# SyncE's transfers wait for the landing of earlier ones: an attention and maxout kernel on one core

## The chip, the core and the metric

The kernel runs on 1 core of one Trainium2 chip. Its time is in device microseconds; the median of 3 runs of the kernel before is 358.42 us (358.3 to 359.15). Five engines work side by side: TensorE (PE, with its weight loads as PEld), VectorE (DVE), ScalarE (ACT), GpSimd (POOL) and SyncE (SP), which here only issues transfers (DMAs).

## The reference

```python
def _attn_ref(q, k, v):                      # 8 batches, 8 heads, 1152 places, 64 wide
    q_pool = q.reshape(B, H, S // 2, 2, D).mean(axis=3)
    scores = scale * np.matmul(q_pool, k.transpose(0, 1, 3, 2))
    scores = scores - np.max(scores, axis=-1, keepdims=True)
    attn = np.exp(scores)
    attn = attn / (np.sum(attn, axis=-1, keepdims=True) + 1e-09)
    return np.matmul(attn, v)

def _moe_ref(x, w1, w2, w_out):              # x: 4608 tokens x 512, d_ff 1024
    return np.maximum(x @ w1, x @ w2) @ w_out
```

The attention's heads are put side by side as x, and the second function's result, 4608 x 512 in float32, is the output.

## The kernel before

The 64 heads are worked in 32 pairs. For each pair three loads of 576 KB come from HBM: q, k and v, each into one of three buffers (`qraw`, `kraw`, `vraw`). GpSimd casts them to bf16 (`cast_k`, `cast_q` with the pooling's addition, `cast_v`). K is turned by TensorE for the first five pairs (`ktrans_pe`) and by a transposing DMA after that (`ktrans`, line 475); the pooled q is turned by TensorE for the first five pairs and by eight VectorE transposes after that (`qtrans_dve`, line 485). TensorE makes the scores (line 302), ScalarE the exponentials (line 317), TensorE the product with V (line 621). The normalized result is turned into `xT`, for most pairs by a transposing DMA (`xtrans`, lines 703 and 712).

The second part works on `xT` while the attention of later pairs goes on. max(a, b) is computed as b + max(a - b, 0): the weights' difference `wd` is made once, the relu of x @ wd comes out of lines 760 and 771, and x @ (w2 w_out) and the relu's product with w_out are added in one accumulation (line 803). The output tiles are stored by `store_p` (lines 829 and 835), the last ones by `store_z` (line 866). The twelve weight blocks of 512 KB are loaded in the opening (`w_load`, line 379), between the loads of the first pairs.

The order of all work is written out by hand in a long string. Each letter is one step: "S" a group of scores, "E" an exponential, "l" the next load of the list `LOADS`, "t" a `ktrans`, "x" an `xtrans`, "o" a store, and so on. `Plan` records the steps with what they read and write, works out which semaphores each has to wait for (`solve`), and emits each engine's instructions in that order. SyncE, too, works in order: an issue that waits holds up everything behind it. `solve` drops a wait for something of which the engine has already been told by an earlier wait.

What an issue on SyncE waits for today: its buffer being free, its data being there (transposes and stores), and, for loads once the exponential steps are past group 42, an exponential two groups back (`pace`). The function `behind` could make a load wait for an earlier load, but its table is empty:

```python
BEHIND = ()
back = [d for at, d in BEHIND if at <= n]
return [f"ld{n - back[-1]}"] if back else [], [f"ld{n}"]
```

So `behind` only gives the load a name, and nobody waits for that name. Two of the pieces in which k of pair 0 is loaded are issued by ScalarE; all other transfers but some of the last stores are SyncE's.

Of the kernel before, what the change touches and what calls it, by code (L numbers as in the profile page):

```python
# [7 lines left out]
P = 128  # L8
# [8 lines left out]
class Plan:  # L17
# [10 lines left out]
    def op(self, eng, fn, r=(), w=(), after=(), dma=None, fence=False, **_):  # L28
        n = len(self.ops)
        for k in r:  # L30
            assert k in self.writer, k
        raw = {self.writer[k] for k in r}
        deps = set(raw)
        for k in tuple(w) + tuple(after):
            if k in self.writer:
                deps.add(self.writer[k])
            deps.update(self.readers.get(k, ()))
        self.ops.append(dict(eng=eng, fn=fn, deps=deps, raw=raw, dma=dma, fence=fence))
        for k in r:
            self.readers.setdefault(k, set()).add(n)  # L40
        for k in w:
            self.writer[k] = n
            self.readers[k] = set()
        return n
# [72 lines left out]
def bass_funnel_attn__then__act_maxout2_kernel(  # L117
# [13 lines left out]
    NT = S // P  # L131
    HP = P // 2
    QU = SQ // HP
    NCH = SQ // P
    NB = SQ - NCH * P
# [22 lines left out]
    W_DIFFS_DVE = ()  # L158
    W_CASTS_POOL = ()
    W_PAIRS = (0, 2)  # L160
    BEHIND = ()
    FILL = 28
    FILLS = 16
    PACE = 2
# [31 lines left out]
    with ctx:  # L196
        def sbuf(shape, dt, name):
            return ctx.enter_context(nc.sbuf_tensor(name, list(shape), dt))
# [12 lines left out]
        kbf = [sbuf([P, NT, 2, D], BF16, f"kbf{s}") for s in range(2)]  # L211
# [20 lines left out]
        osb2 = stage[:, NC_ * F:NC_ * F + 4 * E].rearrange("p (s e) -> p s e", s=4)  # L232
        osb = [osb2[:, s, :] for s in range(4)]
# [12 lines left out]
        op = plan.op  # L246

        def rows(half):
            return slice(half * HP, half * HP + HP)
# [35 lines left out]
        def kkeys(i, lo=0, hi=NT):  # L285
            return [f"kT{i % 3}.{t}" for t in range(lo, hi)]
# [44 lines left out]
            return [f"E{g}"] if PACE and g >= PACE_FROM else []  # L331

        done = [0]
        issued = [0]

        def behind():

            n = issued[0]
            issued[0] += 1
            back = [d for at, d in BEHIND if at <= n]  # L340
            return [f"ld{n - back[-1]}"] if back else [], [f"ld{n}"]

        def load_k(i, lo=0, hi=NT, eng="SP"):
            b, h0, s = i // NHP, 2 * (i % NHP), i % 3
            old, name = behind() if eng == "SP" else ([], [])
            op(eng, lambda e: e.dma_start(  # L346
                kraw[s][:, :, lo:hi, :].rearrange("p h t d -> p h (t d)"),
                k[b, h0:h0 + 2, :, :].rearrange("h (p t) d -> p h (t d)", t=NT)[
                    :, :, lo * D:hi * D]),
                after=([f"kraw0.{c}" for c in K0] if s == 0 and hi - lo == NT else []) + pace() + old,  # L350
                w=([f"kraw0.{lo}"] if hi - lo < NT else [f"kraw{s}"]) + name,
                dma=f"d_kp{lo}" if hi - lo < NT else f"d_k{s}",
                cost=0.2 * (hi - lo) + 0.03 if hi - lo < NT else 1.45 + 0.6 * (i == 1), tag=("L", "k", i))

        def load_q(i, lo=0, hi=QU, eng="SP"):
            b, h0, s = i // NHP, 2 * (i % NHP), i % 3
            old, name = behind() if eng == "SP" else ([], [])
            op(eng, lambda e: e.dma_start(  # L358
                qraw[s][:, lo:hi, :, :].rearrange("p u r d -> p (u r d)"),
                q[b, h0:h0 + 2, :, :].rearrange("h (p r) d -> (h p) (r d)", p=HP)[  # L360
                    :, lo * 2 * D:hi * 2 * D]),
                w=([f"qraw0.{lo}"] if hi - lo < QU else [f"qraw{s}"]) + name,
                after=(["qraw0.0", "qraw0.4"] if s == 0 and hi - lo == QU else []) + pace() + old,
                dma=f"d_qp{lo}" if hi - lo < QU else f"d_q{s}",
                cost=1.45 * (hi - lo) / QU + (0.7 if lo else 0.0), tag=("L", "q", i))

        def load_v(i):
            b, h0, s = i // NHP, 2 * (i % NHP), i % 3
            old, name = behind()
            op("SP", lambda e: e.dma_start(  # L370
                vraw[s][:, :, :, :].rearrange("p h t d -> p h (t d)"),
                v[b, h0:h0 + 2, :, :].rearrange("h (p t) d -> p h (t d)", t=NT)),
                w=[f"vraw{s}"] + name, after=pace() + old, dma=f"d_v{s}", cost=1.48, tag=("L", "v", i))

        def w_load(part, c):
            src, dst, key = ((moe_w2, w2f, "w2f"), (moe_w1, w1f, "w1f"), (moe_w_out, wof, "wof"))[part]
            n = 2 if part == 2 else 1
            old, name = behind()
            op("SP", lambda e: e.dma_start(
                dst[:, c * n:(c + 1) * n, :],  # L380
                src.rearrange("(c p) f -> p c f", p=P)[:, c * n:(c + 1) * n, :]),
                w=[f"{key}{c}"] + name, after=old, dma=f"d_w{part}{c}", cost=1.34, tag=("L", "w", part, c))
# [89 lines left out]

        def ktrans(i):
            s, z = i % 2, i % 3
            op("SP", lambda e: e.dma_start_transpose(
                kT[z][:, :, :], kbf[s][:, :, :, :].rearrange("p t h d -> p (t h d)")),
                r=[f"kbf{s}"], w=kkeys(i), dma=f"d_kT{z}", cost=2.4, mode="t", tag=("kt", i))

        def qtrans_dve(i, n):
            s, z = i % 2, i % 3  # L480
# [202 lines left out]
        def place(b, j):  # L683
            if b % 2 == 0:
                return b * SQ + j * P
            return b * SQ + (NB + j * P if j < NCH else 0)

        def under(cts, n0, n1):
            return [f"{key}{ct}" for ct in cts for key, lo, hi in (
                ("w2b", 512, 1536), ("w2T", 1536, 2560), ("w2f", 2560, NTOK)) if n0 < hi and lo < n1]  # L690

        def xkeys(ct, n0, n1):
            return [f"xT.{ct}.{j}" for j in range(n0 // HP, n1 // HP)]

        def xneed(i, part):
            return [f"{('xn', 'xr')[part]}{i // NHP % 2}.{2 * (i % NHP) + k}" for k in range(2)]

        def xtrans(i, part):

            b, ct = divmod(i, NHP)  # L700
            if part == 0:
                n0 = place(b, 0)
                op("SP", lambda e: e.dma_start_transpose(
                    xT[:, ct, n0:n0 + NCH * P].rearrange("p (j x) -> p j x", x=P),
                    xnat[b % 2][:, ct, :, :].rearrange("p j c -> p (j c)")),
                    r=xneed(i, 0), w=xkeys(ct, n0, n0 + NCH * P), after=under([ct], n0, n0 + NCH * P),
                    dma=f"d_x{ct}{b % 2}", cost=1.2, mode="t", tag=("xt", i, 0))
            else:
                n0 = place(b, NCH)
                cts = [j % NHP for j in rests(i)]  # L710
                c0, c1 = cts[0], cts[-1] + 1
                op("SP", lambda e: e.dma_start_transpose(
                    xT[:, c0:c1, n0:n0 + NB],
                    xend[b % 2][0:NB, c0:c1, :].rearrange("p j c -> p (j c)")),
                    r=sum((xneed(j, 1) for j in rests(i)), []),
                    w=sum((xkeys(c, n0, n0 + NB) for c in cts), []), after=under(cts, n0, n0 + NB),
                    dma=f"d_y{ct}{b % 2}", cost=0.3 * len(cts), mode="t", tag=("xt", i, 1))

        def xtrans_pe(i):
# [102 lines left out]
        def store_p(n):  # L822

            lo, o = n * 2 * P, n % 2 * 2
            todo = []
            for half in range(2):
                (b, u), (b1, u1) = [spot(lo + k * P + half * HP) for k in range(2)]
                if b1 == b and u1 == u + 2:
                    todo.append(lambda b=b, u=u, half=half: op("SP", lambda e: e.dma_start(
                        out[b * SQ:(b + 1) * SQ, :].rearrange("(p u) e -> p u e", u=QU)[:, u:u + 3:2, :],  # L830
                        osb2[rows(half), o:o + 2, :]), r=[f"osb{o}", f"osb{o + 1}"],
                        dma=f"d_o{o}", cost=0.8, tag=("O", n)))
                else:
                    for k, (b, u) in enumerate(((b, u), (b1, u1))):
                        todo.append(lambda b=b, u=u, k=k, half=half: op("SP", lambda e: e.dma_start(
                            out[b * SQ:(b + 1) * SQ, :].rearrange("(p u) e -> u p e", u=QU)[u, :, :],
                            osb[o + k][rows(half), :]), r=[f"osb{o + k}"], dma=f"d_o{o + k}", cost=0.4,
                            tag=("O", n)))
            return todo

        def z_job(lo, c0, c1, o, eng):
# [200 lines left out]
```

## Time and profile before

| | |
|---|---|
| median of 3 runs | 358.42 us (358.3, 358.42, 359.15) |
| span of the profiled execution, first to last instruction | 356.4 us |
| what lies around the span, from the median | 2.0 us |
| busy: PE, ACT, DVE, POOL | 346.0, 313.8, 230.1, 151.4 us |
| TensorE clock granted | 0.999 |
| moved by the DMA engines | 84.55 MB, mean 237 GB/s |
| HBM read and written | 62.91 MB and 9.44 MB |

The profile comes from one execution, and a time of that execution apart from its span is not given; the table sets its span against the median of the runs. In the rows below, "SPq" is SyncE's queue of issues: the second number is how long the issue itself took SyncE, not how long the data took. The time to landing is counted from the start of the issue until all of the data have arrived. "Idle before" an engine's row is put down to what came last.

### The profile page before, as it was taken

Reading aid. Unit: us, or ns where it says so; the run is one execution under the profiler, and the core shown is the slowest. Engines: PE = TensorE matmul, PEld = TensorE weight load, DVE = VectorE, ACT = ScalarE, POOL = GpSimd, SP = SyncE. Lnnn points to the kernel's source line nnn. Section 1 sums busy time; section 2 is a strip of 40 time slices with the busy share of each in tenths; the row PEclk is TensorE's granted clock in tenths of the full one; section 3 lists DMA queues with packets and bytes.
Section 4 is the critical chain, followed back from the end, with each engine's and each line's share of the span. In section 5 each row is a group of like instructions: output and inputs, shape, how many; then the busy total and the mean of one; then the engine's idle time right before and its main releaser. Section 6 shows DMA issues by size and latency. Waiting matters only on the chain.

```text
span 356.4 us, 13757 instructions
## 1 busy us (share of the span) xinstructions
PE 346.0 (97%) x6178; PEld 218.5 (61%) x6178; DVE 230.1 (65%) x472; ACT 313.8 (88%) x354; POOL 151.4 (42%) x136
## 2 busy tenths in 40 slices
PE   7889999999899999999999999999999999999996
PEld 5556665656564675656666576556576757448753
DVE  2587589974966867985887677785586875414001
ACT  5999999999999899999999989989999796992431
POOL 2625997554564264355544455227444621010000
PEclk9999999999999999999999999999999999999999
DMA  8999999999989989998999699998999943012215
GB/s 271 403 397 398 370 255 309 280 289 261 293 252 279 315 196 350 237 301 183 278 320 260 153 230 301 237 314 234 224 299 255 267 68 75 17 32 47 61 31 148
DMA packets 76699, 84.55 MB, mean 237 GB/s; under 512 B 48480, under 2 KB 49760, under 8 KB 76640
## 3 DMA queue, kind: packets, MB, share of 16 engines
q1 hardware_dynamic: 75856, 83.15, 87.5%
q8 instruction: 48, 0.79, 0.9%
q10 hardware_dynamic: 784, 0.52, 0.5%
q14 instruction: 11, 0.09, 0.1%
HBM read 62.91 MB, written 9.44 MB: 203 GB/s over the span
## 4 chain that ended last, share of the span: by engine, by line
PE 87%; ACT 9%; DMA 2%; issue 1%; SPq 0%; DVE 0%
PE ps L803 25%; PE ps L621 20%; PE ps L302 19%; PE ps L760 16%; ACT et L317 9%; PE ps L636 3%; PE ps L593 2%; DMA qraw<-in_q_dram 2%; PE ps L846 1%; PE ps L552 0%; PE ps L533 0%; SPq L346 0%; DVE qp L428 0%; SPq L358 0%; PE ps L730 0%
## 5 line engine op out<-in xcount | busy, mean ns | idle before, releaser
L317 ACT ACTIVATE et<-ps 128x1024 bf16<-128x1024 f32 (+1 forms) x336 | 302.4, 1019 | 14.5 <-PE ps L302 9.7
L302 PE MATMUL ps<-qpT,kT 64*128 64x256 bf16 (+7 forms) x1162 | 117.3, 283 | 2.7 <-issue 1.1
L485 DVE STREAM_TRANSPOSE qpT<-qp 32x288 bf16<-32x288 bf16 x216 | 101.4, 469 | 10.4 <-PE ps L302 6.1
L760 PE MATMUL ps<-xT,wd 64*128 64x512 bf16 (+3 forms) x832 | 81.2, 311 | 0.2
L302 PEld LDWEIGHTS ps<-qpT,kT 64*128 64x128 bf16 x1162 | 48.3, 94 | 49.7 <-ACT et L317 11.3
L803 PE MATMUL ps<-wo,stage 64*128 64x512 bf16 x544 | 76.4, 376 | 0.0
L435 POOL TENSOR_TENSOR qp<-qraw 128x576 bf16<-128x576 f32 x30 | 42.1, 1406 | 61.1 <-DMA qraw<-in_q_dram 57.3
L621 PEld LDWEIGHTS ps<-vE,et 128*128 128x128 bf16 x1728 | 54.9, 97 | 13.9 <-ACT et L317 9.3
L621 PE MATMUL ps<-vE,et 128*128 128x65 bf16 x1728 | 60.7, 193 | 0.7 <-issue 0.3
L771 DVE TENSOR_SCALAR stage<-ps 128x1024 bf16<-128x1024 f32 (+3 forms) x41 | 39.7, 970 | 21.1 <-PE ps L760 20.6
L760 PEld LDWEIGHTS ps<-xT,wd 64*128 64x128 bf16 x832 | 35.6, 94 | 22.2 <-PE ps L760 1.9
L405 POOL TENSOR_SCALAR kbf<-kraw 128x1152 bf16<-128x1152 f32 x31 | 35.7, 1153 | 26.3 <-DMA kraw<-in_k_dram 25.6
L803 PE MATMUL ps<-w,xT 64*128 64x512 bf16 x272 | 40.8, 377 | 0.0
L803 PEld LDWEIGHTS ps<-wo,stage 64*128 64x128 bf16 x544 | 26.4, 94 | 20.5
L445 POOL TENSOR_SCALAR vE<-vraw 128x1152 bf16<-128x1152 f32 x24 | 27.4, 1154 | 19.4 <-PE ps L636 10.8
L809 DVE COPY stage<-ps 128x1024 f32<-128x1024 f32 x14 | 17.1, 1224 | 23.1 <-PE ps L803 23.0
L468 POOL TENSOR_SCALAR stage<-et 128x1152 bf16<-128x1152 bf16 x14 | 16.1, 1152 | 35.5 <-ACT et L317 35.5
L654 DVE TENSOR_TENSOR xnat<-ps,rc 128x256 bf16<-128x256 f32 (+2 forms) x71 | 27.6, 397 | 2.0
L651 DVE RECIPROCAL rc<-ps 128x4 f32<-128x4 f32 (+2 forms) x64 | 11.6, 182 | 25.9 <-PE ps L621 25.5
L621 PEld LDWEIGHTS ps<-stage,et 128*128 128x128 bf16 x576 | 18.1, 97 | 2.7 <-issue 2.6
L621 PE MATMUL ps<-stage,et 128*128 128x65 bf16 x576 | 19.7, 193 | 0.0
L803 PEld LDWEIGHTS ps<-w,xT 64*128 64x128 bf16 x272 | 12.5, 94 | 8.8 <-DVE stage L771 0.2
(55 smaller groups left out, 155.4 us busy)
## 6 DMA issues: line engine op xcount, KB each, us to landing
vraw<-in_v_dram SPq DMA_DIRECT2D x32, 576.0 KB, 6.1
kraw<-in_k_dram SPq DMA_DIRECT2D x31, 576.0 KB, 6.7
qraw<-in_q_dram SPq DMA_DIRECT2D x31, 576.0 KB, 6.3
out_dram<-stage SPq DMA_DIRECT2D x24, 256.0 KB, 4.1
out_dram<-stage SPq DMA_DIRECT2D x21, 128.0 KB, 3.4
xT<-in_moe_w_dram SPq DMA_DIRECT2D x4, 512.0 KB, 12.2
stage<-in_moe_w_out_dram SPq DMA_DIRECT2D x4, 512.0 KB, 14.1
stage<-in_moe_w_dram SPq DMA_DIRECT2D x4, 512.0 KB, 13.2
```

The costliest lines, as they stand in the source:

```text
L302: last = e.matmul(ps[:, h, col:col + hi - lo], kT[i % 3][rows(h), t, :], qpT[i % 3][rows(h), lo:hi], start=True, stop=True)
L317: op("ACT", lambda e: e.activation(et2[:, :, c:c + z - a], ps[:, :, a - g * W:z - g * W], EXP, scale=scale), r=[f"b{m}", f"b{m + 1}"], w=w ...
L405: op("POOL", lambda g: g.tensor_scalar(kbf[s][:, :, :, :].rearrange("p t h d -> p h t d"), kraw[r][:, :, :, :], 1.0, 1.0, ALU.mult, ALU.mu ...
L435: op("POOL", lambda g: g.tensor_tensor(qpf[s][:, :, :], qraw[r][:, :, 0, :], qraw[r][:, :, 1, :], ALU.add), r=[f"qraw{r}"], w=[f"qp{s}.0", ...
L445: return g.tensor_scalar(vE[r][:, :, :, 0:D].rearrange("p t h d -> p h t d"), vraw[s][:, :, :, :], 1.0, 1.0, ALU.mult, ALU.mult)
L485: op("DVE", lambda e: e.transpose(view[dst:dst + 32, :, 32 * pb:32 * pb + 32], qpf[s][src:src + 32, :, 32 * db:32 * db + 32]), r=[f"qp{s}. ...
L621: last = e.matmul(fb[m][:, at * 66:at * 66 + 65], et[:, a:a + P], vE[vs][:, t, half, 0:65], start=(t == 0), stop=(t == NT - 1))
L654: todo.append(evac_op("DVE", lambda e, m, z=z, at=at, num=num, dst=dst: e.tensor_tensor(dst, a(m)[z, at:at + num, 0:D], rc[k][z, at:at + n ...
L760: last = e.matmul(fb[m + k][:, 0:size], wd[z, ct, (f0 + k) * P:(f0 + k + 1) * P], xT[z, ct, n0:n1], start=(turn == 0 and ct == 0), stop=(t ...
L771: return e.tensor_scalar_max(gT[:, f0:f0 + 2, g0:g0 + size], wide[m // 2][:, :, 0:size], 0.0)
L803: last = e.matmul(fb[m + k][:, :], lhs, rhs, start=(turn == 0 and j == 0), stop=(turn == 1 and j == NC_ + NF - 1))
L809: return e.tensor_copy(osb2[:, o:o + 2, :], wide[m // 2][:, :, :])
```

## The change

`behind` gets the cost of the transfer it is asked about, in us (1.45 for a load of q, k or v, 1.29 for a weight block, 1.05 for a transpose of K, 0.5 or 0.25 per block for one of x, 0.67 or 0.36 for a store). It goes back through the line of all earlier transfers of SyncE, adding up costs, its own included. The first one at which the sum passes `LINE` = 5.9 and which is not a store is the one whose landing the new transfer has to wait for. Besides the loads, now the DMA transposes and the stores of `store_p` stand in the line and wait in this way; `store_z` does not. The order of the steps, the buffers and all other work are the same.

```diff
-    BEHIND = ()
+    LINE = 5.9
...
-        issued = [0]
-
-        def behind():
-
-            n = issued[0]
-            issued[0] += 1
-            back = [d for at, d in BEHIND if at <= n]
-            return [f"ld{n - back[-1]}"] if back else [], [f"ld{n}"]
+        line = []
+
+        def behind(cost, store=False):
+
+            name, sent, old = f"dm{len(line)}", cost, []
+            for back, c, stores in reversed(line):
+                sent += c
+                if sent > LINE and not stores:
+                    old = [back]
+                    break
+            line.append((name, cost, store))
+            return old, [name]
...
-            old, name = behind() if eng == "SP" else ([], [])
+            old, name = behind(1.45 * (hi - lo) / NT) if eng == "SP" else ([], [])
...
-            old, name = behind()
+            old, name = behind(1.45)
...
-            old, name = behind()
+            old, name = behind(1.29)
...
         def ktrans(i):
             s, z = i % 2, i % 3
+            old, name = behind(1.05)
             op("SP", lambda e: e.dma_start_transpose(
                 kT[z][:, :, :], kbf[s][:, :, :, :].rearrange("p t h d -> p (t h d)")),
-                r=[f"kbf{s}"], w=kkeys(i), dma=f"d_kT{z}", cost=2.4, mode="t", tag=("kt", i))
+                r=[f"kbf{s}"], w=kkeys(i) + name, after=old, dma=f"d_kT{z}", cost=2.4, mode="t", tag=("kt", i))
...
+                old, name = behind(0.5)
...
+                old, name = behind(0.25 * len(cts))
...
+            def store(dst, src, r, dma, cost):
+                old, name = behind(cost, True)
+                op("SP", lambda e: e.dma_start(dst, src), r=r, w=name, after=old, dma=dma,
+                   cost=cost * 1.2, tag=("O", n))
```

More of the change, by code (lines that the diff above doesn't have):

```diff
@@ L356, in load_q @@
             b, h0, s = i // NHP, 2 * (i % NHP), i % 3
-            old, name = behind() if eng == "SP" else ([], [])
+            old, name = behind(1.45 * (hi - lo) / QU) if eng == "SP" else ([], [])
             op(eng, lambda e: e.dma_start(
@@ L705, in xtrans @@
                     xnat[b % 2][:, ct, :, :].rearrange("p j c -> p (j c)")),
-                    r=xneed(i, 0), w=xkeys(ct, n0, n0 + NCH * P), after=under([ct], n0, n0 + NCH * P),
+                    r=xneed(i, 0), w=xkeys(ct, n0, n0 + NCH * P) + name,
+                    after=under([ct], n0, n0 + NCH * P) + old,
                     dma=f"d_x{ct}{b % 2}", cost=1.2, mode="t", tag=("xt", i, 0))
@@ L715, in xtrans @@
                     r=sum((xneed(j, 1) for j in rests(i)), []),
-                    w=sum((xkeys(c, n0, n0 + NB) for c in cts), []), after=under(cts, n0, n0 + NB),
+                    w=sum((xkeys(c, n0, n0 + NB) for c in cts), name),
+                    after=under(cts, n0, n0 + NB) + old,
                     dma=f"d_y{ct}{b % 2}", cost=0.3 * len(cts), mode="t", tag=("xt", i, 1))
@@ L828, in store_p @@
                 if b1 == b and u1 == u + 2:
-                    todo.append(lambda b=b, u=u, half=half: op("SP", lambda e: e.dma_start(
+                    todo.append(lambda b=b, u=u, half=half: store(
                         out[b * SQ:(b + 1) * SQ, :].rearrange("(p u) e -> p u e", u=QU)[:, u:u + 3:2, :],
-                        osb2[rows(half), o:o + 2, :]), r=[f"osb{o}", f"osb{o + 1}"],
-                        dma=f"d_o{o}", cost=0.8, tag=("O", n)))
+                        osb2[rows(half), o:o + 2, :], [f"osb{o}", f"osb{o + 1}"], f"d_o{o}", 0.67))
                 else:
                     for k, (b, u) in enumerate(((b, u), (b1, u1))):
-                        todo.append(lambda b=b, u=u, k=k, half=half: op("SP", lambda e: e.dma_start(
+                        todo.append(lambda b=b, u=u, k=k, half=half: store(
                             out[b * SQ:(b + 1) * SQ, :].rearrange("(p u) e -> u p e", u=QU)[u, :, :],
-                            osb[o + k][rows(half), :]), r=[f"osb{o + k}"], dma=f"d_o{o + k}", cost=0.4,
-                            tag=("O", n)))
+                            osb[o + k][rows(half), :], [f"osb{o + k}"], f"d_o{o + k}", 0.36))
             return todo
```

## The prediction

> **What bounds the kernel now.** I read the page first (busy shares, slices, chain), then the busy times by stage, then who waited for whom, then SyncE's timeline with the landing of single transfers.
>
> ```profile
> span 356.4 us, 13757 instructions
> PE 346.0 (97%) x6178; PEld 218.5 (61%) x6178; DVE 230.1 (65%) x472; ACT 313.8 (88%) x354; POOL 151.4 (42%) x136
> DMA  8999999999989989998999699998999943012215
> PE 87%; ACT 9%; DMA 2%; issue 1%; SPq 0%; DVE 0%
> vraw<-in_v_dram SPq DMA_DIRECT2D x32, 576.0 KB, 6.1
> kraw<-in_k_dram SPq DMA_DIRECT2D x31, 576.0 KB, 6.7
> qraw<-in_q_dram SPq DMA_DIRECT2D x31, 576.0 KB, 6.3
> xT<-in_moe_w_dram SPq DMA_DIRECT2D x4, 512.0 KB, 12.2
> stage<-in_moe_w_out_dram SPq DMA_DIRECT2D x4, 512.0 KB, 14.1
> stage<-in_moe_w_dram SPq DMA_DIRECT2D x4, 512.0 KB, 13.2
> ```
>
> PE works 346.0 of 356.4 us: it leaves 10.4 us in all that any change to the transfers could win. The DMA engines look full too (nines nearly to slice 32), but the chain that ended last has 2% of DMA against 87% of PE. The last number of each transfer row is the median time from issue to landing, and it holds the fact that this change turns on: the loads of the long middle land some 6 us after their issue, the weights of the opening 12 to 14 us after it. So the line is much deeper in the opening than later. The next view gives PE's idle time by stage (columns: length, PE, PEld, DVE, ACT, POOL, then the clock, DMA share and GB/s).
>
> ```profile
> 0.00:9.00 9.00, 6.53 (x92) 5.16 (x92) 2.47 (x8) 4.97 (x6) 1.82 (x11) 1.00 0.81 272
> 9.00:25.00 16.00, 13.70 (x306) 8.18 (x302) 10.72 (x17) 15.57 (x18) 8.32 (x7) 1.00 1.04 398
> 25.00:45.00 20.00, 19.48 (x392) 12.29 (x394) 13.87 (x24) 19.57 (x24) 14.01 (x13) 1.00 1.00 383
> 45.00:60.00 15.00, 14.59 (x250) 8.08 (x246) 13.08 (x28) 14.99 (x18) 13.72 (x12) 1.00 1.16 283
> 60.00:290.00 230.00, 228.47 (x4150) 145.51 (x4152) 171.15 (x361) 220.94 (x247) 110.10 (x92) 1.00 1.04 260
> 290.00:357.00 67.00, 63.23 (x1002) 39.28 (x994) 18.78 (x37) 37.79 (x47) 3.46 (x3) 0.99 0.25 59
> ```
>
> From 60 to 290 us PE idles 1.5 us in 230. From 9 to 60 us ACT is the fuller engine (idle 0.4, 0.4 and 0.0 us). Before 9 us everything waits for the first loads, and after 290 us there are no loads (59 GB/s). So the loads can decide the time in the opening alone, up to about 46 us, where they run at 383 to 398 GB/s. Who waits for them:
>
> ```profile
> POOL qp L435 <- DMA qraw<-in_q_dram: 57.3, 22, 6.2
> POOL kbf L405 <- DMA kraw<-in_k_dram: 25.6, 15, 3.5
> POOL stage L445 <- DMA vraw<-in_v_dram: 10.2, 6, 4.4
> PEld ps L302 <- ACT et L317: 11.3, 48, 0.5
> DVE qpT L485 <- POOL qp L435: 0.8, 3, 0.3
> DVE xT L498 <- DMA xT<-in_moe_w_dram: 0.7, 2, 0.4
> SPq L475 <- POOL kbf L405: 11.9, 2, 10.7
> ```
>
> GpSimd's casts wait for loads all the time (57.3 + 25.6 + 10.2 us), yet DVE, which takes what they make, waits for them 0.8 us in the whole run, and no row of PE or ACT names kT or xT landing late. A load that lands a little later in the middle costs GpSimd time it has (42% busy). In the opening the cover is thin: DVE's weight casts (L498) start when their load lands.
>
> **Part 1: the waits in the opening.** The rule adds up the costs of the transfers ahead until the sum passes 5.9. With 1.45 for a load and 1.29 for a weight block, four later ones fit (4 x 1.45 = 5.8), so a transfer waits for the landing of the fourth or fifth ahead. SyncE's opening today:
>
> ```profile
> 2.24 0.47 SPq L358 DMA_DIRECT2D qraw<-in_q_dram  x1
> 2.75 0.43 SPq L346 DMA_DIRECT2D kraw<-in_k_dram  x1
> 3.23 0.94 SPq L358 DMA_DIRECT2D qraw<-in_q_dram  x2
> 10.84 5.89 SPq L379 DMA_DIRECT2D stage<-in_moe_w_out_dram  x3
> 23.96 4.05 SPq L358 DMA_DIRECT2D qraw<-in_q_dram  x2
> 31.96 0.71 SPq L346 DMA_DIRECT2D kraw<-in_k_dram  x1
> 43.38 1.50 SPq L475 DMA_TRANSPOSE kT<-kbf  x1
> ```
>
> Issue to landing, one row for each: the q load of 2.24, the q load of 26.8 (the second of the pair at 23.96), the k load of 31.96, and for comparison the v load issued at 243.3, ahead of which in the line was only a transpose issued 4.4 us before it:
>
> ```profile
> DMA to landing us min/median/max: 5.9/5.9/5.9
> DMA to landing us min/median/max: 13.3/13.3/13.3
> DMA to landing us min/median/max: 14.8/14.8/14.8
> DMA to landing us min/median/max: 4.1/4.1/4.1
> ```
>
> The fourth transfer lands at 2.24 + 5.9 = 8.1 us and the 31st at 31.96 + 14.8 = 46.8: 27 transfers in 38.7 us, 1.43 us each. So the k load issued at 31.96 has about 14.8 / 1.43 = 10 transfers in the line. SyncE runs far ahead, until the line itself stops it: three weight issues take 5.89 us of its queue.
>
> After the change the first transfer held is the second q load of the pair at 3.23; from there on all 25 up to 31.96 are, the last ones by some 8 us. For the last k load the fourth ahead is the q load of 26.8, which lands at 26.8 + 13.3 = 40.1: it is issued at 40.1 instead of 31.96. What is queued behind it on SyncE is the transpose at 43.38, and that one waits until then for GpSimd's cast anyway (the 10.7 us in the last row of the waits). So the late issue delays nothing behind it.
>
> What it does to landings: when a transfer is released, the three or four ahead of it still have 4 x 1.43 - 1.43 = 4.3 us or more of the line's work, and an unhindered load needs 4.1 us from issue to landing, 1.4 of them its own data. Its data are wanted by the line after 4.3 us, and it needs 4.1 - 1.4 = 2.7 us to begin: 1.6 us of cover. The line's order is the same and it does not run dry, so landings stay where they are. Cost of this part: 0, hidden by those 1.6 us; without them, see the first rival. A gain is excluded before 9 us, because the loads that the opening waits for (those at 0.8 to 3.23) are issued before any wait.
>
> **Part 2: the middle.** The loads land 6.1 to 6.7 us after issue, 4 to 5 transfers at 1.43: the line already stands at the depth that the rule sets, because buffers and exponentials pace the issues. Stepping through all 208 issues that the diff touches with the landing times of the trace, 11 of the later ones would be held, by 0.1 to 1.1 us. The longest, the v load issued at 134.09, would wait for the v load issued at 128.87; their issues and landings:
>
> ```profile
> 128.87 0.63 SPq L370 DMA_DIRECT2D vraw<-in_v_dram  x1
> DMA to landing us min/median/max: 6.3/6.3/6.3
> 134.09 0.44 SPq L370 DMA_DIRECT2D vraw<-in_v_dram  x1
> DMA to landing us min/median/max: 8.1/8.1/8.1
> ```
>
> It is released at 128.87 + 6.3 = 135.2 and lands, as now, at 134.09 + 8.1 = 142.2, since from 135.2 it needs only 4.1 us (139.3). Behind it on SyncE stand a q load, a k load and the transpose of a K; each is in the same position. If the whole 1.1 us did reach the landing, GpSimd would take it, and DVE's 0.8 us of waiting in the whole run shows how seldom that gets further. Cost: 0; bounds 0 and the two places where issues are held in a row (about 134 and 175 us, 1.1 and 0.8 us), so 1.9 us.
>
> **Part 3: the wait instructions.** Up to some 200 waits are added to SyncE, fewer where the planner already knows a landing. The price of one that is met shows in the gap ahead of an issue:
>
> ```profile
> 5.75 0.94 SPq L379 DMA_DIRECT2D xT<-in_moe_w_dram  x2
> 6.81 0.38 SPq L346 DMA_DIRECT2D kraw<-in_k_dram  x1
> ```
>
> The k load at 6.81 waits for the casts of pair 0, long done then: 6.81 - 5.75 - 0.94 = 0.12 us of gap. The k load at 2.75 above has no wait and a gap of 2.75 - 2.24 - 0.47 = 0.04 us. So a met wait costs at most 0.08 us, for some six issues per pair of heads 0.5 us on a queue that then waits for ACT again. It does not add up from pair to pair. The stores of the end get a wait on transfers landed long ago, under 0.1 us each, and the last stores (L866) are not touched. Cost to the end: 0 to 0.1 us, and I take 0.1.
>
> **The sum.** 0 + 0 + 0.1 us: the span stays at 356.4 to 356.5. The median of the runs shown is 358.42, 2.0 us above the profiled span; with that difference kept, 358.5, and I forecast no change: 358.5 us. About 0.3% (1.1 us) is what a measurement of this kernel can tell from no change.
>
> **Rivals.** *Four are too few (slower).* The place is the opening, the mechanism a round trip longer under load than the 4.1 us of the quiet line; it decides from the point where issue to landing exceeds four times 1.43 = 5.7 us. If it were the 6.3 us that q loads take at the median, each transfer would cost 6.3 / 4 = 1.58 instead of 1.43, 0.15 us more; over the some 16 transfers that land up to 32 us and feed weight casts and the first heads that is 2.3 us. ACT has 0.9 us of idle time from 9 to 45 us, so nearly all of it would reach the end: 358.4 + 2.3 = 360.7. For it: DVE's weight cast waits for its load today. Against it: the 6.3 us contain the time behind other loads, at the very depth in question. The Trainium skill (DMA: Bandwidth & Descriptors, Latency and other measured facts) has the memory's latency at 0.2 us on average and 2 us at high load; an estimate by it adds 1.8 us to the quiet 4.1, 5.9 in all, and would put the line just past the point of this rival. No run here shows that latency by itself. The same page's rule for authors to issue early and wait late also speaks for this rival. I give it 0.15.
>
> *The held issues of the middle come through (slower).* The two rows of held issues pass their 1.9 us to the landing of q, and GpSimd's in-order queue passes them to DVE's transposes and these to PE: 358.4 + 1.9 = 360.3. Against it stand 0.8 us of DVE waits; 0.07.
>
> *A shallow line serves better (faster).* Ten transfers in the line might slow the one at its head, or stop SyncE when something urgent comes. It could win part of the 2.3 us that PE idles from 9 to 25 us, say half: 358.4 - 1.2 = 357.2. For it: the issues of up to 5.89 us. Against it: nothing urgent stands in SyncE's queue before 43.38, the order is the same, and 398 GB/s is the highest rate of any stage; 0.12.
>
> *The change does nothing* because the planner drops the waits: in the opening SyncE has waited for almost nothing, so it cannot; it would give the forecast's time anyway.
>
> **How the numbers follow.** No change has 0.66 and lies within 1.1 us, 357.4 to 359.5 with the spread of the runs. The slower rivals have 0.22, the faster 0.12. The range goes from 357.2, the faster rival's time, to 360.7, the first rival's: it leaves out what lies beyond them, under 0.2.
>
> **What would show it.** Right: the issues from 3.7 to 32 us drawn out to 40 us, the weights landing some 6 us after issue instead of 12 to 14, no issue of 5.89 us any more; the last load of the opening still landing near 46.8 us, 383 to 398 GB/s from 9 to 45 us, PE's idle time by stage as above. Wrong in the first way: fewer GB/s from 9 to 45 us and DVE's and GpSimd's casts waiting longer there. Wrong in the second: more than 0.8 us of DVE waiting for qp, and PE idle after 60 us. Wrong in the third: PE over 13.7 us busy from 9 to 25 us with less filling.

## The result, and the profile after

The changed kernel is slower: 360.82 us at the median (359.82 to 362.68) against 358.90 us for the kernel before in the same measurement (357.99 to 359.21). The ratio is 1.0061 with a 95% interval of [1.0038, 1.0084]: about +2.2 us by the ratio, +1.9 us by the two medians. The ratios here and below leave out executions in the chip's slower state (one of "line74" and one of "middle2"), and so they are not exactly the quotients of the medians. The time is the first rival's (360.7), not the forecast's (358.5). A second measurement of the same changed kernel, "after2" below, gave 1.0035 [1.0005, 1.0065]. The profiled execution took 360.82 us at a span of 358.8; as before, 2.0 us lie around the span.

The page of the kernel after (head, summary of the chain of waits, and issues with their median time to landing):

```profile
span 358.8 us, 13826 instructions
PE 345.7 (96%) x6177; PEld 218.5 (61%) x6178; DVE 229.9 (64%) x472; ACT 313.9 (88%) x354; POOL 151.5 (42%) x136
PE 81%; DMA 11%; ACT 5%; issue 1%; POOL 0%; DVE 0%; SPq 0%
vraw<-in_v_dram SPq DMA_DIRECT2D x32, 576.0 KB, 6.0
kraw<-in_k_dram SPq DMA_DIRECT2D x31, 576.0 KB, 6.3
xT<-in_moe_w_dram SPq DMA_DIRECT2D x4, 512.0 KB, 6.2
stage<-in_moe_w_out_dram SPq DMA_DIRECT2D x4, 512.0 KB, 5.8
stage<-in_moe_w_dram SPq DMA_DIRECT2D x4, 512.0 KB, 6.2
```

The weights land some 6 us after issue instead of 12 to 14, as foreseen. PE's work is the same (345.7 us). What is new is DMA's share of the chain that ended last: 11% instead of 2%. The chain in order of time shows where (start, duration, what; the long pieces up to 60 us):

```profile
1.28 3.50 DMA kraw<-in_k_dram
4.80 7.15 DMA qraw<-in_q_dram
11.96 6.59 DMA xT<-in_moe_w_dram
18.57 5.98 DMA vraw<-in_v_dram
24.56 5.94 DMA qraw<-in_q_dram
30.52 6.19 DMA stage<-in_moe_w_dram
36.73 5.73 DMA qraw<-in_q_dram
42.52 1.41 POOL qp L439
45.91 13.43 ACT et L317 x15
```

This is the change at work. Each load starts where the one before it ends: the landing of one releases the issue of the next. The same view of the kernel before has nothing of the kind there; from 9 us on it runs through the exponentials, with short pieces of TensorE's work between the two long rows:

```profile
2.24 5.91 DMA qraw<-in_q_dram
9.43 15.70 ACT et L317 x17
44.70 13.43 ACT et L317 x15
```

Each link of the new chain moves the line on by four transfers, which SyncE's timeline lets one count (start, duration, and the issues in a row without idle time between):

```profile
18.57 0.38 SPq L374 DMA_DIRECT2D vraw<-in_v_dram  x1
20.01 3.46 SPq L383 DMA_DIRECT2D stage<-in_moe_w_out_dram  x3
24.56 0.34 SPq L362 DMA_DIRECT2D qraw<-in_q_dram  x1
...
42.47 0.37 SPq L350 DMA_DIRECT2D kraw<-in_k_dram  x1
45.20 2.10 SPq L480 DMA_TRANSPOSE kT<-kbf  x1
```

From the v load at 18.57 to the q load at 24.56 there are four issues (the v load and three weight blocks). The five links from 11.96 to 42.46 us are 30.5 us for twenty transfers: 1.53 us each on average, where the kernel before took 1.43. The last load of the opening is issued at 42.47 and lands 7.0 us later:

```profile
DMA to landing us min/median/max: 7.0/7.0/7.0
```

That is 49.4 us instead of 46.8, and the transpose behind it is issued at 45.20 instead of 43.38. By stage (columns as in the prediction):

```profile
9.00:25.00 16.00, 12.70 (x297) 7.89 (x296) 10.13 (x15) 15.56 (x18) 7.50 (x7) 1.00 1.00 361
25.00:45.00 20.00, 18.30 (x368) 11.41 (x368) 12.68 (x23) 18.57 (x21) 13.12 (x11) 1.00 1.01 371
45.00:60.00 15.00, 14.71 (x264) 8.50 (x262) 12.93 (x29) 14.68 (x17) 14.65 (x14) 1.00 1.13 302
60.00:290.00 230.00, 227.42 (x4137) 144.79 (x4134) 171.28 (x360) 220.12 (x246) 109.79 (x92) 1.00 1.04 262
```

The rate falls from 398 and 383 to 361 and 371 GB/s. The DMA share goes from 1.04 and 1.00 to 1.00 and 1.01: it counts the time of packets, not bytes, and says little of the loss. ACT, the fuller engine up to 60 us, is busy 53.97 us by then (5.16 from 0 to 9 us, with 15.56 + 18.57 + 14.68) against 55.10 before (4.97 + 15.57 + 19.57 + 14.99): 1.1 us lost. Most of the rest of the 2.4 us between the two spans is in PE's busy time from 60 to 290 us, 227.42 against 228.47. Who waited for whom:

```profile
DVE qpT L490 <- POOL qp L439: 2.6, 2, 2.0
PE ps L302 <- issue: 2.1, 1, 2.1
DVE wo L503 <- DMA stage<-in_moe_w_out_dram: 0.9, 2, 0.7
```

DVE's longest wait for q (2.0 us) lies in the opening, behind the q load that the chain shows at 36.73. So the sign that the prediction named for its second rival (over 0.8 us of DVE waiting for qp) appears, but from the opening. The wait of PE that ends on nothing shown ("issue") is one of 2.1 us near 93 us; it was 1.1 us before. The experiments come back to it.

### The profile page after: what moved, and what is told of

Read it like the earlier page. It is cut to its first block, busy times and chain, and to the rows that moved or that the text cites. A ratio compares the mean times of both kernels' runs of the same rounds, so it can differ in the third digit from the quotient of the medians.

```text
span 358.8 us, 13826 instructions
## 1 busy us (share of the span) xinstructions
PE 345.7 (96%) x6177; PEld 218.5 (61%) x6178; DVE 229.9 (64%) x472; ACT 313.9 (88%) x354; POOL 151.5 (42%) x136
## 4 chain that ended last, share of the span: by engine, by line
PE 81%; DMA 11%; ACT 5%; issue 1%; POOL 0%; DVE 0%; SPq 0%
PE ps L812 25%; PE ps L626 19%; PE ps L302 18%; PE ps L769 16%; DMA qraw<-in_q_dram 5%; ACT et L317 5%; PE ps L641 3%; DMA xT<-in_moe_w_dram 2%; DMA stage<-in_moe_w_dram 2%; DMA vraw<-in_v_dram 2%; PE ps L859 1%; DMA kraw<-in_k_dram 1%; POOL qp L439 0%; PE ps L557 0%; DVE qpT L490 0%
## 5 line engine op out<-in xcount | busy, mean ns | idle before, releaser
L626 PEld LDWEIGHTS ps<-vE,et 128*128 128x128 bf16 x1728 | 54.8, 97 | 13.4 <-ACT et L317 9.0
L449 POOL TENSOR_SCALAR vE<-vraw 128x1152 bf16<-128x1152 f32 x24 | 27.3, 1153 | 20.3 <-DMA vraw<-in_v_dram 11.0
```

Of the source, the lines that this page charges most:

```text
L449: return g.tensor_scalar(vE[r][:, :, :, 0:D].rearrange("p t h d -> p h t d"), vraw[s][:, :, :, :], 1.0, 1.0, ALU.mult, ALU.mult)
L626: last = e.matmul(fb[m][:, at * 66:at * 66 + 65], et[:, a:a + P], vE[vs][:, t, half, 0:65], start=(t == 0), stop=(t == NT - 1))
```

## The experiments

Theory A, after the result: a transfer is released only when its last piece has landed, under load that takes over four times 1.43 us, and so four outstanding transfers starve the line in the opening. The rivals: the loss comes from the middle, from the waiting instructions themselves, or from the wait of PE near 93 us.

**One part alone.** "opening" holds only the first 31 transfers, "middle" only the later ones; "middle2" is the same kernel as "middle", measured anew. The edit of "opening" is shown; in "middle" the condition is `31 <= len(line) < 1000000`.

```diff
-                if sent > LINE and not stores:
+                if sent > LINE and not stores and 0 <= len(line) < 31:
```

> The waits of the change hold only the first 31 transfers of SyncE (up to the last load of the opening); later ones have none. Theory A (the loss is made in the opening: a transfer is released by the last of its sixteen DMA engines, the engines that are 2 us ahead of it run dry, and the stalls that the deep line hid reach the landings): the last load of the opening lands 2 to 3 us later than its 46.7 us, 9 to 45 us run at 360 to 375 GB/s, and the kernel is slower by 1.2 to 2.0 us, nearly all of what the whole change cost. Rival B (the held issues of the middle, or SyncE's time for the waits): landings of the opening late but absorbed, the kernel slower by 0.3 us at most.

> The waits of the change hold only transfers after the first 31; the opening is issued as before. Theory A: opening as before (last load at 46.7 us, 383 to 398 GB/s), the kernel within 0.3 us of before. Rival B: slower by 1.5 to 2 us, PE idle after 60 us.

> The middle alone at 5.9 again, with more runs, since 0.5 us with an interval from 0 to 1.1 us did not settle it. Theory A: 0 to 0.4 us. Rival B: 0.5 to 1.0 us, clear of nothing.

Measured: opening 1.0022 [1.0001, 1.0042] (359.37 us against 358.55); middle 1.0015 [0.9997, 1.0032] (359.27 against 358.55), and anew 0.9999 [0.9970, 1.0028] (359.17 against 358.52). The stages of the kernel "opening":

```profile
9.00:25.00 16.00, 14.72 (x294) 8.76 (x293) 10.09 (x15) 15.00 (x17) 7.08 (x7) 1.00 0.98 356
25.00:45.00 20.00, 19.48 (x406) 12.15 (x401) 13.69 (x26) 19.94 (x24) 12.85 (x11) 1.00 1.02 382
```

and its chain of waits from 9 us on, which is the same ladder of landings:

```profile
12.72 6.88 DMA kraw<-in_k_dram
19.62 6.12 DMA stage<-in_moe_w_out_dram
25.76 5.53 DMA stage<-in_moe_w_out_dram
31.30 6.69 DMA kraw<-in_k_dram
38.02 6.11 DMA kraw<-in_k_dram
```

The kernel "middle" has the opening of before, on its first stage:

```profile
9.00:25.00 16.00, 14.30 (x298) 8.36 (x298) 10.58 (x17) 15.28 (x18) 8.30 (x7) 1.00 1.04 400
```

So the slow line comes with the hold in the opening and with nothing else. The last load of "opening" lands at 49.4 us, 2.6 us late, as expected; its rates (356 and 382 GB/s) lie just outside the expected 360 to 375. In time, the opening alone costs some 0.8 us (the interval goes from near 0 to 1.5), less than the 1.2 to 2.0 expected; the middle costs at most 0.3%, and both of its intervals include no change.

**The waiting instructions without the hold.** LINE = 20 keeps the machinery and lets some fourteen transfers be outstanding.

```diff
-    LINE = 5.9
+    LINE = 20.0
```

> The change with 20 in place of 5.9: the same names, and waits for a transfer some fourteen ahead, which has landed long before except for a moment in the opening, so that nearly nothing is held. Theory A: within 0.3 us of before. Rival C (not the depth costs, but the wait instructions and what the planner makes of them): slower by 1 to 2 us, as the whole change is.

> 20 in place of 5.9 again, the only variant whose median (357.96 us) was under that of the kernel before (358.55 us), with an interval on both sides of no change. If waits that hold almost nothing change nothing: within 0.3 us of before, and its opening as deep as before (weights landing 12 to 15 us after issue). If a bounded but deep line is truly better: faster by 0.5 us or more, clear of nothing.

Measured: 0.9989 [0.9963, 1.0015] and, for the same kernel anew, 1.0020 [0.9998, 1.0041]. The first looked a little faster, the second a little slower; both include no change, and the weights of the opening land 12 to 15 us after issue as before. The waits cost nothing that shows.

**One more outstanding.** LINE = 7.4 adds one load to the line.

> The change with 7.4 in place of 5.9: five transfers outstanding instead of four, one more at 1.43 us. Theory A: an unhindered round trip of 4.1 us and the 2.1 us by which the last engine lands after the first are 6.2 us, less than five times 1.43 = 7.15, so most of the loss is gone: at most 0.5 us slower than before, last load of the opening under 1 us late. Rival D (any limit on the depth costs about the same, since the line served ten deep is served faster): slower by 1.5 us or more, 9 to 45 us still under 375 GB/s.

Measured: 1.0003 [0.9986, 1.0021]. Its first two stages, its weights, and the issue and landing of the last load of the opening:

```profile
9.00:25.00 16.00, 14.10 (x307) 8.40 (x307) 10.85 (x17) 15.63 (x18) 8.02 (x7) 1.00 1.04 399
25.00:45.00 20.00, 19.58 (x408) 12.46 (x407) 13.86 (x24) 19.84 (x24) 13.89 (x13) 1.00 1.00 382
```

```profile
stage<-in_moe_w_out_dram SPq DMA_DIRECT2D x4, 512.0 KB, 7.0
```

```profile
38.61 0.37 SPq L350 DMA_DIRECT2D kraw<-in_k_dram  x1
```

```profile
DMA to landing us min/median/max: 8.1/8.1/8.1
```

The hold is plain to see (weights 7.0 us after issue; last load issued at 38.61 instead of 31.96), yet the rate is that of before and the load lands at 46.7, as before. Five outstanding transfers do what the prediction said that four would do.

**The changed kernel again, and fewer outstanding.** "after2" is the changed kernel. "open44" (LINE = 4.45, the first 31 transfers) leaves three outstanding in the opening, "mid44" (LINE = 4.45, the later ones) three in the middle.

> The changed kernel again, unaltered, with more runs, so that it stands on the same chip as its parts. Holding the opening alone cost 0.8 us and holding the middle alone 0.5 us (that one not clear of nothing). If the two add up and nothing else is in it: slower by 1.0 to 1.6 us, 0.3 to 0.45%. If the parts feed each other (a late opening leaves the middle less slack): 2 us or more.

> 4.45 in place of 5.9, so three outstanding, and only for the first 31 transfers. Theory A (a round trip holds the unhindered 4.1 us and the spread of the engines, some 2 us): a transfer of the opening takes up to 6.1 / 3 = 2.0 us instead of 1.43, and no less than 1.7 if the spread shrinks to 1 us; the last load of the opening lands 6 to 14 us late, the kernel is slower by 4 to 12 us. Rival Q (the spread plays no part, only the unhindered 4.1 us): 4.1 / 3 = 1.37 is under 1.43, so three are about as good as four: last load at most 3 us late, slower by at most 1 us.

> 4.45 in place of 5.9, three outstanding, only for transfers after the first 31. Theory A with the middle's cover as the prediction had it (nothing that PE needs is late by less than some us): within 0.5 us of before, although far more issues are held. Rival B (what is held in the middle comes through): clearly more than the 0.5 us that holding at 5.9 showed, 1.5 us or more, with PE idle between 60 and 290 us and DVE waiting for qp for over 3 us.

Measured: after2 1.0035 [1.0005, 1.0065], open44 1.0203 [1.0151, 1.0255], mid44 1.0123 [1.0086, 1.0159]. after2 is about 1.25 us slower, which fits parts that add up; the first measurement (+2.2 us) fits parts that feed each other. The runs do not decide between the two. The first stage of open44, and issue and landing of its last load of the opening:

```profile
9.00:25.00 16.00, 12.73 (x261) 7.63 (x260) 8.54 (x13) 14.41 (x16) 6.83 (x6) 0.97 0.88 297
```

```profile
49.12 0.37 SPq L350 DMA_DIRECT2D kraw<-in_k_dram  x1
```

```profile
DMA to landing us min/median/max: 5.7/5.7/5.7
```

297 GB/s, and the last load lands at 54.8 us, 8.1 us late: fewer outstanding, slower line, as theory A has it, and rival Q (at most 3 us late) is out. Not all of the time need be the loads': TensorE's granted clock is 0.97 in this stage, and in two of the four runs it is 0.986 over the whole; the one run at 1.00 took 364.82 us, 6.3 us more than the median of before. With mid44 the theory missed: it expected 0.5 us at most and the middle lost 4.4 us, with DVE waiting 3.8 us for qp, as rival B has it. The middle has cover for four outstanding transfers, not for three.

**What a transfer takes from issue to release.** The trace records the completion of each transfer sixteen times, once for each DMA engine, and its waiting instruction needs all sixteen. Worked out from these records for the 25 transfers of the opening from the seventh on (medians in us; "us per transfer" is the mean from the seventh landing to the 31st; a step is the time from one landing to the next, counted up to the 31st landing from the fifth on):

```
kernel (outstanding)   issue to first   issue to last   first to last   us per     steps of        last load
                       engine           engine          engine          transfer   1.9 or more     lands at
before (about ten)     10.96            13.12           2.13            1.43       1               46.7
line74 (five)           4.98             7.05           2.05            1.47       2               46.7
after  (four)           3.94             5.98           2.08            1.56       5               49.4
after2 (four)           4.15             6.25           2.13            1.60       7               50.3
opening (four)          4.17             6.20           2.15            1.59       5               49.4
open44 (three)          3.57             5.21           1.62            1.78       9               54.8
```

The quiet v load of 243.3 had its first engine done 3.27 us after issue and its last 4.09 us after, 0.8 us apart. With four outstanding the first engine is done after 3.9 to 4.2 us, so 0.7 to 0.9 us later than in the quiet line, and the last one some 2.1 us behind it. 6.0 to 6.25 us for four is 1.50 to 1.56 each, more than the 1.43 that the line can do; five fit (7.05 / 5 = 1.41), three are far off (5.21 / 3 = 1.74). In the deep line the engines are as far apart (2.13 us), but nobody waits for that. The loss is not spread evenly: the median step is 1.43 us before and 1.44 and 1.45 us in the two profiles of the changed kernel, and what it loses lies in the few long steps, of up to 2.7 us.

**A stall of one engine.** To see whether delays of single engines add up in a line that waits for the slowest, a transfer of 17 rows (34 KB) that runs on one engine (it leaves two completions in the trace, the others sixteen) was put behind the 13th transfer, in the kernel before ("one_before") and in the changed one ("one_after", "one_after2"). Its data are not used.

```diff
+        def one_engine():
+            op("SP", lambda e: e.dma_start(
+                xnat[1][0:17, 0:2, :, :].rearrange("p a b c -> p (a b c)").bitcast(FP32), moe_w_out[0:17, :]),
+                w=[f"xn1.{h}" for h in range(8)], dma="d_one", cost=0.1)
...
+                if c == "l" and len(sp_line["l"]) == LEFT:
+                    simple["s"].pop(0)()
```

> The kernel before, with one more transfer put into SyncE's line behind the 13th: 34 KB in 17 rows, which go over a single DMA engine and keep it busy some 1.4 us longer than the other fifteen (the data are not used). Theory A (the deep line hides a stall of one engine, since the others do not wait for it and another engine is last anyway): the first engine of each transfer lands as before, the last load of the opening lands within 0.3 us of the 45.9 to 47.2 us seen in the four profiles with a deep opening. Rival E (a stall of one engine delays the landings whatever the depth): all landings from there on 1.0 to 1.4 us later, the load of weights ahead of the last load at 45.3 to 45.7 instead of 44.1 to 44.4 us.

> The changed kernel with the same extra transfer behind the 13th. Theory A (four outstanding: the late engine holds the release of the transfer four behind, and all sixteen engines with it): first and last engine of the transfers from the 18th on land 0.7 to 1.4 us later than in the two profiles of the changed kernel (there the 18th, a weight block, lands at 28.5 and 28.8 us, the last load at 49.4 and 50.3 us). Rival E: the same shift in both kernels. Rival F (a stall of one engine plays no part in either): no shift over 0.5 us.

> The same kernel once more for a second profile, since the landings of the opening differ by up to 0.9 us between the two profiles of the changed kernel. Theory A as before: the mean of the two 0.7 to 1.4 us later than the mean of the two without the extra transfer.

Measured: 0.9997 [0.9936, 1.0058], 1.0047 [0.9983, 1.0111] and 1.0026 [0.9958, 1.0093]; the landings say more. In the kernel before, the last load landed at 46.58, as expected of a stall that is hidden, and as it would without one. In the changed kernel nothing was added either: the 18th transfer landed at 28.1 us in both against 28.5 and 28.8 without, the last load at 48.9 and 48.2 against 49.4 and 50.3. The expectation failed. In "one_after" the small transfer was done at 20.59, between the first engine (18.73) and the last (20.66) of its neighbour: it seems to have taken an engine that had time. So this experiment doesn't show single stalls adding up; what stands is the spread of about 2.1 us itself.

The traces hold candidates of their own, though. The instruction queue (`q8 instruction` on the page) moves 16 KB in a single packet of 1.0 to 1.4 us every 4 to 9 us of the opening. In the kernel before, by the second landing after each of its packets at 12.4, 20.3, 26.5, 32.8 and 40.1 us one more engine is over 1.3 us behind the first (from one engine to six), and the landing itself does not move; only the packet at 44.2 is followed by a long step (2.4 us). In the changed kernel the packets at 10.9, 25.2, 32.0 and 46.0 us are followed within three landings by four of the five long steps (2.7, 2.0, 2.3 and 2.7 us), those at 20.0 and 36.6 us by none. This is read from the times alone; no run tested it.

**The wait of PE near 93 us.** It measured 1.1 us before and 2.1 after, but also 1.1 in opening, line74 and open44, 1.2 in mid44, 1.4 and 1.5 in middle and middle2, 0.9 in line20, and 1.1 and 1.3 in the changed kernel with the extra transfer. The changed kernel's second profile has no such wait of PE on that line; its PE is busy 229.21 us from 60 to 290. So the 1 us that this wait added in the first profile isn't tied to the change. The intervals of the two measurements (+0.6% and +0.35%) overlap; whether this wait has a part in the difference was not shown.

## Why the prediction was wrong

**Part 1, the opening, is the step that failed.** It was costed at 0, under "1.6 us of cover": when a transfer is released the line has 4.3 us of work left, and a load "needs 4.1 - 1.4 = 2.7 us to begin". The 4.1 us came from a load that had the line almost to itself, and the line was treated as one pipe. Held at four, a load took 6.0 to 6.25 us from issue to its last engine (medians), so 4.5 to 4.8 us "to begin" where the prediction had 2.7, and the line had 4.3 us of work: not 1.6 us of cover but 0.3 to 0.5 us short in every four, on average. About 0.8 us of the difference is in the first engine and 1.3 us in the spread between the engines, of which the last one releases the next issue. This sum is the rate told in another way; that the limit is the cause is shown by the runs, with the loss gone at five outstanding and at twenty in LINE, and larger at three. (By the rule it is always the fourth transfer ahead that is waited for, not the fourth or fifth, since a transfer's own cost counts in the sum.) From it follow the other misses of this part: the last load was to be issued at 40.1 and went at 42.5; it was to land near 46.8 and landed at 49.4 and 50.3; 383 to 398 GB/s became 361 and 371. "The late issue delays nothing behind it" fell with it: the transpose went from 43.38 to 45.20.

**How much reaches the end.** The last load of the opening lands 2.7 and 3.6 us late in the two profiles of the changed kernel, and the time grew by 2.2 and 1.3 us. ACT's busy time in the first 60 us is 53.3 to 54.7 us in the five profiles with four outstanding in the opening (53.97, 53.32, 53.61, 53.33, 54.72; mean 53.8) and 54.4 to 55.4 in the eight with five or more (mean 54.9): about 1.1 us, which agrees with the 0.8 us that holding the opening alone cost.

**Part 2, the middle**, was costed at 0 with a bound of 1.9 us, and at four outstanding the runs agree as far as they can tell (1.0015 and 0.9999, at most 0.3%). mid44 shows the edge one step further on, at three.

**Part 3, the waits,** held: line20 stays within no change.

**The gain before 9 us** was excluded, and none came from the change: the loads up to 3.23 us go out as before. PE is busy 7.32 us up to 9 us where the profile of before has 6.53, but 7.49 and 7.20 in middle and middle2, whose opening is not held.

**The first rival** had the place, the condition (a round trip over 5.7 us) and the size per transfer: 6.3 / 4 = 1.58 us against 1.53 to 1.60 measured. That its time, 360.7 us, lies so near 360.8 and 360.3 is in part luck: it let nearly all of its 2.3 us reach the end, and of the 2.6 us by which "opening" lands late about 0.8 us did. It got 0.15 because of the argument that "the 6.3 us contain the time behind other loads, at the very depth in question". That was the wrong way round: at a limit of four, time behind three other loads is part of the round trip. The median of the middle, where four to five were outstanding already, was the nearest row for a line held at four, and the 4.1 us of a quiet line the farthest. The trace of before also held the second half: in its deep line first and last engine were 2.13 us apart.

**The estimate from the Trainium skill** (DMA: Bandwidth & Descriptors, Latency and other measured facts), 5.9 us, came close in sum to the 6.0 to 6.25 measured. The records can't tell whether the memory's latency is in it. Against the quiet load the first engine is 0.7 to 0.9 us later and the last 1.9 to 2.2, so more than half of the difference is spread between the engines. That fits another section of the same page of the Trainium skill (Why a DMA increments its semaphore by 16 and not by 1), by which the engines of one transfer finish independently and only the full count says that all is there.

**Open:** whether the packets of the instruction queue are what sets the engines apart and makes the long steps, why the spread is some 2.1 us with four outstanding as with ten (and 1.6 with three), and the size of the one wait near 93 us. A release by the first engine was not tried, since its data need not all be there.

## What to carry to other kernels

To bound the outstanding transfers, divide the time from issue to the landing of the last engine, measured under load at about that depth, by the time per transfer of the full line, and round up: here 6.2 / 1.43 gives five, and four cost 0.3 to 0.6%. The quiet transfer's time is too short a measure, and the quotient holds only for the depth at which it was taken: with three outstanding it gives four (5.2 / 1.43 = 3.6), which was too few, and in the deep line ten (13.1 / 1.43 = 9.2), which is more than needed. So measure once more at the limit that it gives. Where loads are the pace, as in this opening, read GB/s and the chain in order of time: a ladder of loads, each starting where another ends, is a line that waits for itself.

## What was not expected of the hardware

The sixteen engines of one transfer finish some 2.1 us apart under load, with ten outstanding as with four, and 0.8 us apart in the quiet load. A line of three, four, five and about ten transfers of 512 to 576 KB moved 297, 361, 399 and 398 GB/s in the same stretch, while the DMA share read 0.88, 1.00, 1.04 and 1.04: between four and five the share says 4% and the bytes say 10%.
